# Copies of hash bits and later loads of K, Q and V issued from GpSimd's queue instead of SyncE's

## The chip, the cores and the metric

The kernel runs on one core of a Trainium2 chip. The metric is the device time of one execution in microseconds (us). A core has five engines that work side by side, each through its own list of instructions in order: PE (TensorE, matrix products), DVE (VectorE), ACT (ScalarE), POOL (GpSimd) and SP (SyncE, which here only issues DMA transfers). A DMA is issued by one engine's queue, which first waits for whatever the transfer needs, and is then carried out by 16 DMA engines beside the others. PSUM is the accumulator memory of PE, SBUF the core's main memory.

## The reference

Attention with a mask from hashing, then a two-layer network with an ELU. A score counts only where the six hash bits of the query's and the key's projection agree.

```python
def _attn_ref(q, k, v, proj):          # q, k, v: 4 x 8 x 768 x 64, proj: 64 x 6
    q_bits = (np.einsum('bhsd,dk->bhsk', q, proj) > 0)
    k_bits = (np.einsum('bhsd,dk->bhsk', k, proj) > 0)
    ...
    mask = q_bucket[:, :, :, None] == k_bucket[:, :, None, :]
    scores = scale * np.matmul(q, k.transpose(0, 1, 3, 2))
    scores = np.where(mask, scores, -1000000000.0)
    scores = scores - np.max(scores, axis=-1, keepdims=True)
    attn = np.exp(scores)
    attn = attn / (np.sum(attn, axis=-1, keepdims=True) + 1e-09)
    return np.matmul(attn, v)
...
def _moe_ref(x, w_in, w_out):          # x: 3072 x 512, w_in: 512 x 2048, w_out: 2048 x 512
    h = x @ w_in
    g = np.where(h > 0.0, h, np.exp(np.minimum(h, 0.0)) - 1.0)
    return g @ w_out
```

## The kernel before

**Numbers.** PE multiplies 16-bit floats, so each float32 operand is scaled and split into a high and a low half (`hi`, `lo`), and a product is made of three matmuls or of stacked halves. The weights arrive as 64-bit floats and are decoded in integer steps.

**Units of work.** There are 4 batches of 8 heads. Two heads are a *pair*; a batch is cut into two *chunks* of 3 x 128 query rows, so there are 8 chunks with 4 pairs each, 32 pairs in all. A pair has 6 *slots*, one for each of its two heads and three blocks of 128 queries. The main loop runs over the 192 slots. In each slot PE makes one block of scores (`scores`, L508), DVE takes its maximum on the way out of PSUM (L520, tile `pt`), ACT takes the exponential (L536), ACT and DVE split it into halves (`hl`, L143 and L152), and SP issues a DMA transpose of it into `PT` (L551). Four slots after its last block a pair's product with V runs on PE (`attend`, L559). Beside it runs the network of the chunk before: `h` (L585), its ELU (L596 to L600, tiles `U`), and `o` (L621); at a chunk's end three results are scaled out of PSUM and stored by GpSimd (L635).

**Preparing a pair.** Its Q, and at a batch's first chunk its K too, goes through these steps, each due a set number of slots ahead of the pair's first slot (`PREP`, or `PREP0` for the first four pairs): loads from HBM (`kst` L305, `qst` L344; V is loaded in L391 as `vf`), a sum of squares on ACT that sets the scale (L207), the split (`natk`, `nat1q`, `nat2q`), and DMA transposes on SP into `K1` (L328), `O1` and `O2` (L371, L372). Then `project`: DVE copies the high half of K1 into K2 (L162), PE multiplies by the hash matrix (L286), DVE compares with a threshold (L291, tile `zb`), and the bits are copied by small DMAs of 12 rows x 384 elements into spare rows of K2 (four copies) and O2 (two copies): `bits`, L295. A matmul over these rows then adds the mask to the scores. The traces write K for K1 and K2 and O for O1 and O2.

**What sets the order.** The code emits steps in the order of their due slots. A scheduler at compile time puts them on each engine's list by priority, buffer by buffer and by its own idea of when inputs are there; from slot 30 on PE's list alone is kept as written. Every DMA but the stores and the two loads of the hash matrix stands in SP's list: loads, bits, transposes of K, Q and P, and the weights at the start.

Of the kernel before, what the change touches and what calls it, by code (L numbers as in the profile page):

```python
# [66 lines left out]
def lsh_attention_moe(  # L67
# [10 lines left out]
    nc = tc.nc  # L78
    B, H, S, D = q.shape
    NB = proj.shape[1]  # L80
# [4 lines left out]
    NP = H // 2  # L85
    HALF = S // 2
# [7 lines left out]
    QD = 32  # L94
# [151 lines left out]
    def spare(a, b, dt=F32):  # L246
# [2 lines left out]
        free[0] -= n  # L249
        return Wf[:, free[0] : free[0] + n].bitcast(dt).rearrange("p (a b) -> p a b", b=b)  # L250

    class Stage:


# [21 lines left out]
    def flat(t):  # L276
        return t.rearrange("p a b -> p (a b)")

    def bits(o, ways, w, which):

        t = ps_a.tile([P, 512], F32, tag="av", name="z")[:, :w]
        quads = len(ways[0][1])
        for n, (x, moving) in enumerate(ways):
            for u, mv in enumerate(moving):
                rows = mv.shape[0]
                nc.tensor.matmul(  # L286
                    t[u * QD : (u + 1) * QD], pj["z"][:rows, x, :], mv, start=n == 0, stop=n == len(ways) - 1
                )
        zb = small.tile([P, HALF], F16, tag="zb", name="zb", bufs=2)[:, :w]
        used = slice(0, quads * QD)  # L290
        nc.vector.tensor_scalar(  # L291
            zb[used], t[used], pj["thr"][used, which : which + 1], (MBIT, -MBIT)[which], ALU.is_gt, ALU.mult
        )
        for u in range(quads):
            d = nc.sync.dma_start(o[D : D + 2 * NB, u * w : (u + 1) * w], zb[u * QD : u * QD + 2 * NB])  # L295
        return d

    kexs = {}
# [1 line left out]
    def prep_k(b, ps, sts, sgs):  # L300
        def load():
            with after(0, "first") if b == 0 and "first" in ks[0, 0] else nullcontext():
                for p, st, sg_ in zip(ps, sts, sgs):
                    st["kf"] = stg.tile([P, 2 * NC, D], F32, tag="k", name="kst", bufs=2) if sg_.kf is None else sg_.kf
                    nc.sync.dma_start(  # L305
                        st["kf"].rearrange("p (h c) d -> p h (c d)", h=2),
                        k[b, 2 * p : 2 * p + 2].rearrange("h (p c) d -> p h (c d)", c=NC),
                    )

        def scale():  # L310
            w = len(ps)
            mx = small.tile([P, 2], F32, tag="kx", name="kx")[:, :w]
            for n, (st, sg_) in enumerate(zip(sts, sgs)):
                squares(mx[:, n : n + 1], flat(st["kf"]), sg_.k1)
            yield
            if b not in kexs:
                kexs[b] = small.tile([P, NP], F32, tag="ke", name="ke", bufs=2)
            _, sc = powers(mx, w, 4.0, QK_TOP, "k", squares=True, ex=kexs[b][:, ps[0] : ps[0] + w])
            for n, st in enumerate(sts):
                st["ksc"] = sc[:, n : n + 1]  # L320

        def split(st, sg_):
            s, nat = st["ksc"], sg_.k1
            scaled("n_hi", nat[:, :, :D], st["kf"], s)
            rest("n_lo", nat[:, :, D:], st["kf"], s, nat[:, :, :D])
            st["K1"] = okp.tile([P, 2 * NC, P], F16, tag="K1", name="K1", bufs=NP)
            st["K2"] = okp.tile([P, 2 * NC, P], F16, tag="K2", name="K2", bufs=NP)
            st["first"] = nc.sync.dma_start_transpose(st["K1"], flat(nat))  # L328

        def project(st):  # L330
            k1, k2 = flat(st["K1"]), flat(st["K2"])
            copied("dup", k2[:D], k1[:D])
            quads = [k1[:, u * HALF : (u + 1) * HALF] for u in range(4)]
            st["done"] = bits(k2, ((0, quads), (1, quads)), HALF, 0)

        return load, scale, split, project

    def prep_q(b, c0, nc_, ps, ksts, sts, sgs):
        def load():
            with after(0, "first") if b == 0 and "first" in ks[0, 0] else nullcontext():  # L340
                for p, st, sg_ in zip(ps, sts, sgs):
                    st["qf"] = stg.tile([P, 2 * HC, D], F32, tag="q", name="qst", bufs=2) if sg_.qf is None else sg_.qf
                    st["qf"] = st["qf"][:, : 2 * nc_, :]
                    nc.sync.dma_start(  # L344
                        st["qf"].rearrange("p (h c) d -> p h (c d)", h=2),
                        q[b, 2 * p : 2 * p + 2].rearrange("h (p c) d -> p h (c d)", c=NC)[:, :, c0 * D : (c0 + nc_) * D],
                    )

        def scale():
            w = len(ps)  # L350
            mx = small.tile([P, 2], F32, tag="qx", name="qx")[:, :w]
            for n, (st, sg_) in enumerate(zip(sts, sgs)):
                squares(mx[:, n : n + 1], flat(st["qf"]), sg_.q1[:, : 2 * nc_])
            yield
            ex, sc = powers(mx, w, 4.0, QK_TOP, "q", rows=True, squares=True)
            sg = small.tile([P, 2, 2], F32, tag="sg", name="sg")
            c = D**-0.5 * 2.0 ** (-2 * QK_TOP)
            for x in range(2):
                nc.vector.scalar_tensor_tensor(
                    sg[:, x, :w], ex, c if x == 0 else -c, kexs[b][:, ps[0] : ps[0] + w], ALU.mult, ALU.mult  # L360
                )
            for n, st in enumerate(sts):
                st["qsc"], st["sg"] = sc[:, n : n + 1], sg[:, :, n]

        def split(st, sg_):
            s, nat1, nat2 = st["qsc"], sg_.q1[:, : 2 * nc_, :], sg_.q2[:, : 2 * nc_, :]
            scaled("n_hi", nat1[:, :, :D], st["qf"], s)
            rest("n_lo", nat2[:, :, :D], st["qf"], s, nat1[:, :, :D])
            copied("dup", nat1[:, :, D:], nat1[:, :, :D])
            st["O1"], st["O2"] = o_ring.take(2 * nc_, (b, c0))  # L370
            nc.sync.dma_start_transpose(st["O1"], flat(nat1))  # L371
            nc.sync.dma_start_transpose(st["O2"], flat(nat2))  # L372

        def project(st):
            w = nc_ * P
            o1, o2 = flat(st["O1"]), flat(st["O2"])
            hi, lo = ([x[:, u * w : (u + 1) * w] for u in range(2)] for x in (o1, o2[:D]))
            st["made"] = bits(o2, ((2, hi), (2, lo), (3, lo)), w, 1)

        return load, scale, split, project  # L380


    def prep_v(b):
        st = {"f": [], "v": [None] * NP}

        def load():
            mx = small.tile([P, NP], F32, tag="vx", name="vx")
            for p in range(NP):
                f = vpool.tile([P, 2, NC, D], F32, tag="v", name="vf")
                with tc.issue_after(ks[b, V_AFTER]["done"].ins) if b == 0 else nullcontext():  # L390
                    nc.sync.dma_start(  # L391
                        f.rearrange("p h c d -> p h (c d)"),
                        v[b, 2 * p : 2 * p + 2].rearrange("h (p c) d -> p h (c d)", c=NC),
                    )
                st["f"].append(f)
            st["mx"] = mx
            if b == 0:
                for p in range(NP):
                    sums(p)
# [288 lines left out]
    ks, qs = {}, {}  # L688

    def prep(ns):  # L690

        c = chunks[pairs[ns[0]][0]]
        ps = [pairs[n][1] for n in ns]
        b = c["b"]
        for n in ns:
            qs[n] = {}
        sgs = [stages[n % STAGES] if n < NP else steady for n in ns]
        ksts = [ks.setdefault((b, p), {}) for p in ps]
        parts = [(prep_q(b, c["c0"], c["nc"], ps, ksts, [qs[n] for n in ns], sgs), [qs[n] for n in ns])]
        if c["c0"] == 0:  # L700
            parts.insert(0, (prep_k(b, ps, ksts, sgs), ksts))

        def load():
            for part, _ in parts:
                part[0]()

        made = []

        def sums():
            made.extend(part[1]() for part, _ in parts)  # L710
            for m in made:
                next(m)

        def scale():
            with behind_max():
                for m in made:
                    next(m, None)

        def split(i):
            for part, sts in parts:  # L720
                part[2](sts[i], sgs[i])

        def project(x, i):
            part, sts = parts[x]
            part[3](sts[i])

        return load, sums, scale, split, project, len(parts)
# [7 lines left out]
    for ns in groups:  # L735
        early = ns[0] < NP
        lead = [begin[ns[0]] - x for x in (PREP0 if early else PREP)]
        split_at = []
        for n in ns:
            at = begin[n] - (PREP0 if early else PREP)[2]  # L740

            w = 2 * chunks[pairs[n][0]]["nc"]
# [61 lines left out]
    done = 0  # L804
# [84 lines left out]
    for G in range(starts[-2] + 1):  # L889
        if G == starts[0]:  # L890
            ordered.enter_context(tc.manual_schedule(engines={mybir.EngineType.PE}))
        if G < len(slots):
            n, at = slots[G]
# [61 lines left out]
```

## Time and profile before

| | |
|---|---|
| time, median of 3 runs | 952.47 us (951.82 to 953.67) |
| the profiled execution | 948.24 us, of it the span 946.5 us |
| PE busy, share of the span | 818.4 us, 86% |
| ACT busy | 739.3 us, 78% |
| DVE busy | 704.0 us, 74% |
| POOL busy | 15.7 us, 2% |
| SP's DMA queue, share of 16 engines | 68.9%, 131.25 MB |
| GpSimd's DMA queue | 1.9%, 6.29 MB |

A busy time is the sum of an engine's instructions; waits and the issuing of DMAs are not in it. A row of the timeline reads: start in us from the span's start, duration, engine, line, operation, tile written and tiles read, count; in brackets the idle time before it and what ended it. "SPq" is the queue of SP: its rows are issues, and the time of a row is how long the issue held the queue. A merged row (x2, x4) contains any waits between its members. A row of the waits reads: waiting engine, tile and line, releaser, then total us, times, longest. In a row that gives a line's instructions the three durations are minimum, median and maximum in ns. The first 160 us or so are the head, in which the weights are loaded and decoded and the first chunk's attention runs; then the network of one chunk runs beside the attention of the next, until about 860 us, and the last chunk's network ends the kernel.

### The profile page before, as it was taken

How to read it: one execution, taken by the hardware profiler on the slowest of the kernel's cores; microseconds unless marked ns; L12 is line 12 of the kernel's file. 1: busy time of each engine (PE TensorE's matmuls, PEld its weight loads, DVE VectorE, ACT ScalarE, POOL GpSimd, SP SyncE). 2: the span in 40 equal slices, each digit the busy share in tenths (PEclk: the TensorE clock that was granted, in tenths of full speed). 3: DMA queues.
4: the chain of work that ended last, by engine and by line, in shares of the span. 5: the costliest groups of instructions: out<-in, count | busy, mean ns of one | idle time of the engine just before them, and what ended most of it. 6: DMA issues, size and time to landing. Idle time of an engine off the chain costs nothing.

```text
span 946.5 us, 14531 instructions
## 1 busy us (share of the span) xinstructions
PE 818.4 (86%) x4975; PEld 420.4 (44%) x4975; DVE 704.0 (74%) x1528; ACT 739.3 (78%) x1469; POOL 15.7 (2%) x49
## 2 busy tenths in 40 slices
PE   2536555888999999988998999998999999999996
PEld 0113222444545555444544455544545555555553
DVE  6899899898867877678777687787878687674332
ACT  4677777999879888789779788889888788885442
POOL 1000000000000000000000000000000000000000
PEclk9956666998999999999999999999999999999998
DMA  9999886776887767696886767795777667556000
GB/s 280 280 207 224 226 231 161 136 141 145 153 167 169 153 113 126 132 187 117 163 180 137 139 109 150 148 181 101 144 155 136 118 119 151 102 101 100 34 1 35
DMA packets 404586, 138.47 MB, mean 146 GB/s; under 512 B 380960, under 2 KB 398880, under 8 KB 404512
## 3 DMA queue, kind: packets, MB, share of 16 engines
q1 hardware_dynamic: 402432, 131.25, 68.9%
q0 software_dynamic: 1920, 6.29, 1.9%
q8 instruction: 39, 0.64, 0.3%
q14 instruction: 35, 0.29, 0.1%
q10 hardware_dynamic: 160, 0.00, 0.0%
HBM read 35.65 MB, written 6.29 MB: 44 GB/s over the span
## 4 chain that ended last, share of the span: by engine, by line
issue 50%; DVE 14%; PE 14%; DMA 13%; ACT 6%; SPq 1%; POOL 1%; POOLq 0%; ACTq 0%; DVEq 0%
PE o L621 4%; PE av L559 4%; PE h L585 3%; DVE pt L520 3%; DMA PT<-hl 3%; DVE hl L152 3%; PE s L508 2%; DMA K<-natk 2%; DMA O<-nat1q 2%; ACT pt L536 2%; DMA W<-in_moe_w_in_dram 1%; DMA U<-in_moe_w_out_dram 1%; DVE W L469 1%; POOL out_dram L635 1%; DVE W L479 1%
## 5 line engine op out<-in xcount | busy, mean ns | idle before, releaser
L621 PE MATMUL o<-W,U 128*128 128x512 f16 x1152 | 280.2, 380 | 3.2 <-ACT W L143 3.1
L585 PE MATMUL h<-x,W 128*128 128x384 f16 x1536 | 279.8, 326 | 0.0
L585 PEld LDWEIGHTS <-W 128*128 128x128 f16 x1536 | 147.5, 98 | 111.1 <-issue 9.9
L536 ACT ACTIVATE pt<-pt,nb,sg 128x768 f32<-128x768 f32 x192 | 195.3, 1019 | 1.7
L152 DVE SCALAR_TENSOR_TENSOR hl<-pt,r,hl 128x768 f16<-128x768 f32 x192 | 189.4, 1011 | 7.5 <-ACT hl L143 7.2
L520 DVE TENSOR_SCALAR_CACHE_REDUCE pt<-s 128x768 f32<-128x768 f32 x177 | 168.0, 949 | 22.9 <-PE s L508 21.9
L143 ACT ACTIVATE hl<-pt,r 128x768 f16<-128x768 f32 x192 | 168.7, 927 | 20.2 <-DVE r L546 19.4
L508 PE MATMUL s<-K,O 128*128 128x384 f16 x708 | 153.3, 340 | 32.2 <-DVE pt L520 26.9
L621 PEld LDWEIGHTS <-U 128*128 128x128 f16 x1152 | 111.0, 98 | 122.7 <-issue 8.9
L559 PE MATMUL av<-PT,vhl 128*64 128x384 f16 x1152 | 115.6, 350 | 27.3 <-DMA PT<-hl 20.8
L600 DVE SCALAR_TENSOR_TENSOR U<-U 128x384 f32<-128x384 f32 x128 | 70.9, 554 | 85.8 <-ACT U L599 84.8
L508 PEld LDWEIGHTS <-O 76*128 76x128 f16 (+1 forms) x768 | 74.7, 102 | 134.7 <-issue 51.2
L596 ACT ACTIVATE U<-h,ch 128x384 f32<-128x384 f32 x128 | 72.9, 570 | 63.7 <-PE h L585 63.6
L152 DVE SCALAR_TENSOR_TENSOR U<-U,sgg 128x384 f16<-128x384 f32 x128 | 78.4, 612 | 53.3 <-ACT U L143 53.3
L559 PEld LDWEIGHTS <-vhl 128*64 128x64 f16 x1152 | 72.8, 117 | 81.7 <-ACT hl L143 17.7
L143 ACT ACTIVATE U<-U,sgg 128x384 f16<-128x384 f32 x128 | 77.8, 608 | 20.5 <-DVE U L600 20.4
L599 ACT ACTIVATE U<-h,ch 128x384 f32<-128x384 f32 x128 | 72.9, 570 | 0.0
L472 PE MATMUL acc<-W,ones 128*128 128x512 bf16 x32 | 16.9, 546 | 35.7 <-DVE W L469 35.5
L536 ACT ACTIVATION_READ_ACCUMULATOR pt<-pt,nb,sg 128x1 f32 x192 | 36.4, 190 | 0.0
L533 ACT ACTIVATE nb<-m,sg 128x2 f32<-128x2 f32 x96 | 27.7, 289 | 6.8 <-DVE pt L520 6.4
L291 DVE TENSOR_SCALAR zb<-z,pjt 64x384 f16<-64x384 f32 (+1 forms) x48 | 29.1, 606 | 3.9 <-PE z L286 3.9
L207 ACT ACTIVATE nat1q<-qst 128x384 bf16<-128x384 f32 x30 | 15.5, 516 | 18.1 <-DMA O<-nat1q 16.0
(103 smaller groups left out, 527.2 us busy)
## 6 DMA issues: line engine op xcount, KB each, us to landing
U<-in_moe_w_in_dram SPq DMA_DIRECT2D x12, 512.0 KB
vf<-in_v_dram SPq DMA_DIRECT2D x16, 384.0 KB
U<-in_moe_w_out_dram SPq DMA_DIRECT2D x12, 512.0 KB
out_dram<-W POOLq DMA_DIRECT2D x24, 256.0 KB, 4.0
qst<-in_q_dram SPq DMA_DIRECT2D x30, 192.0 KB
kst<-in_k_dram SPq DMA_DIRECT2D x14, 384.0 KB
PT<-hl SPq DMA_TRANSPOSE x192
W<-in_moe_w_in_dram SPq DMA_DIRECT2D x4, 512.0 KB
```

The lines of the kernel that those rows point to most:

```text
L143: nc.scalar.activation(o, x, AF.Copy, scale=s)
L152: nc.vector.scalar_tensor_tensor(o, x, s, hi, ALU.mult, ALU.subtract)
L291: nc.vector.tensor_scalar(zb[used], t[used], pj["thr"][used, which : which + 1], (MBIT, -MBIT)[which], ALU.is_gt, ALU.mult)
L508: nc.tensor.matmul(s_tile[:, n, :HALF], st[o][:rows, at, :], kst[kk][:rows, j * NC + n * HC : j * NC + (n + 1) * HC, :].rearrange("p a b - ...
L520: top = nc.vector.tensor_scalar(pt.rearrange("p (n e) -> p n e", n=2), s_tile[:, :, :HALF], CLAMP, None, ALU.max, ALU.max, accum_out=duo[0 ...
L536: nc.scalar.activation(pt, pt, AF.Exp, bias=nb[:, n : n + 1], scale=st["sg"][:, 0:1], accum_out=sm[:, n : n + 1])
L559: nc.tensor.matmul(av[j * D : (j + 1) * D], vt[:, j, c, vx, :], PTs[j][:, :, px, c, :], start=n == 0, stop=n == last,)
L585: nc.tensor.matmul(h, WH[:, g * KT + t, wx, fc * P : (fc + 1) * P], c["xs"][t][:, xx, :], start=n == 0, stop=n == 3 * KT - 1,)
L596: nc.scalar.activation(e, h, AF.Exp, scale=c["ch"])
L599: nc.scalar.activation(hp, h, AF.Relu, scale=c["ch"])
L600: nc.vector.scalar_tensor_tensor(e, e, -1.0, hp, ALU.add, ALU.min)
L621: nc.tensor.matmul(o[t][:, :DO], g16[:, gx, t * P : (t + 1) * P], WH[:, NSI + 1 + f, wx, :], start=f == 0 and i == 0, stop=f == NF - 1 and ...
```

## The change

DMAs of three kinds get another issuing queue, GpSimd's in place of SP's: the copies of hash bits, the loads of K and Q, and the loads of V. The first chunk's pairs (n < 4, and K and V of batch 0) keep SP. Nothing is computed differently, and sizes and buffers stay. The new lines make line numbers behind them three higher.

```diff
+    def queue_of(st):
+        return nc.sync if st["early"] else nc.gpsimd
+
...
-    def bits(o, ways, w, which):
+    def bits(o, ways, w, which, queue):
...
-            d = nc.sync.dma_start(o[D : D + 2 * NB, u * w : (u + 1) * w], zb[u * QD : u * QD + 2 * NB])
+            d = queue.dma_start(o[D : D + 2 * NB, u * w : (u + 1) * w], zb[u * QD : u * QD + 2 * NB])
...
-                    nc.sync.dma_start(
+                    queue_of(st).dma_start(
                         st["kf"].rearrange("p (h c) d -> p h (c d)", h=2),
...
-            st["done"] = bits(k2, ((0, quads), (1, quads)), HALF, 0)
+            st["done"] = bits(k2, ((0, quads), (1, quads)), HALF, 0, queue_of(sts[0]))
...
-                    nc.sync.dma_start(
+                    queue_of(st).dma_start(
                         st["qf"].rearrange("p (h c) d -> p h (c d)", h=2),
...
-            st["made"] = bits(o2, ((2, hi), (2, lo), (3, lo)), w, 1)
+            st["made"] = bits(o2, ((2, hi), (2, lo), (3, lo)), w, 1, queue_of(sts[0]))
...
-                    nc.sync.dma_start(
+                    (nc.gpsimd if b else nc.sync).dma_start(
                         f.rearrange("p h c d -> p h (c d)"),
...
-            qs[n] = {}
+            qs[n] = {"early": n < NP}
...
-        ksts = [ks.setdefault((b, p), {}) for p in ps]
+        ksts = [ks.setdefault((b, p), {"early": b == 0}) for p in ps]
```

Since the scheduler orders every engine's list anew, the change moves more than the DMAs. SP's list before, in the second batch, where the third and the fourth of its K tiles are transposed (K_2496 and K_2795 are K1 of its third and fourth pair, K_2176 the K2 of its second; O_ are the Q tiles):

```order
L328 DMA_TRANSPOSE K_2496<-natk 128x12x128
L551 DMA_TRANSPOSE PT<-hl 128x12x128 x2
L295 DMA K_2176<-zb 12x384 x4
L295 DMA O_2182<-zb 12x384 x2
L328 DMA_TRANSPOSE K_2795<-natk 128x12x128
L344 DMA qst<-in_q_dram 128x2x192 x2
L305 DMA kst<-in_k_dram 128x2x384
L551 DMA_TRANSPOSE PT<-hl 128x12x128 x2
L371 DMA_TRANSPOSE O_2801<-nat1q 128x6x128
L372 DMA_TRANSPOSE O_2802<-nat2q 128x6x128
```

The same place of SP's list in the changed kernel:

```order
L331 DMA_TRANSPOSE K_2496<-natk 128x12x128
L554 DMA_TRANSPOSE PT<-hl 128x12x128 x2
L331 DMA_TRANSPOSE K_2795<-natk 128x12x128
L554 DMA_TRANSPOSE PT<-hl 128x12x128 x2
L374 DMA_TRANSPOSE O_2801<-nat1q 128x6x128
```

The six bits copies and the three loads around the transpose of K_2795 are gone from this queue. GpSimd's list held only the 24 stores after its start; in the changed kernel it has at this place:

```order
L298 DMA K_2176<-zb 12x384 x4
L347 DMA qst<-in_q_dram 128x2x192
L298 DMA O_2182<-zb 12x384 x2
L308 DMA kst<-in_k_dram 128x2x384
L394 DMA vf<-in_v_dram 128x2x384
L298 DMA K_2497<-zb 12x384 x4
L638 DMA out_dram<-W 128x512 x2
L298 DMA O_2503<-zb 12x384 x2
L638 DMA out_dram<-W 128x512
```

Copies, loads and stores now stand in one line, and O_2503's copies stand between a chunk's stores. On DVE the same place before, from the split of the fourth pair's K (natk) to the copy into its K2 (K_2796):

```order
L152 SCALAR_TENSOR_TENSOR natk<-kst,ks,natk 128x12x64
L600 SCALAR_TENSOR_TENSOR U<-U 128x384
L546 RECIPROCAL r<-r 128x2
L520 TENSOR_SCALAR pt,m<-s 128x768
L152 SCALAR_TENSOR_TENSOR U<-U,sgg 128x384
L152 SCALAR_TENSOR_TENSOR hl<-pt,r,hl 128x768 x2
L600 SCALAR_TENSOR_TENSOR U<-U 128x384
L642 SCALAR_TENSOR_TENSOR ch<-ve,w0e 128x1
L162 COPY K_2796<-K_2795 64x1536
```

And in the changed kernel:

```order
L152 SCALAR_TENSOR_TENSOR natk<-kst,ks,natk 128x12x64
L549 RECIPROCAL r<-r 128x2
L152 SCALAR_TENSOR_TENSOR U<-U,sgg 128x384
L523 TENSOR_SCALAR pt,m<-s 128x768
L152 SCALAR_TENSOR_TENSOR hl<-pt,r,hl 128x768 x2
L162 COPY K_2796<-K_2795 64x1536
L603 SCALAR_TENSOR_TENSOR U<-U 128x384
L645 SCALAR_TENSOR_TENSOR ch<-ve,w0e 128x1
```

The copy, which needs the transpose of K_2795, has moved ahead of the second U (L600 before, L603 now) and of ch, and the first U has moved ahead of natk.

## The prediction

> **What bounds the kernel now.** I read the page first, for which engine is full in which stretch; then the busy time of each engine in four stretches, which puts a ceiling on any gain; then the waits; then single places in the timeline. The stretches (start and end, then busy us and instructions of each engine, the clock granted to PE, DMA share and GB/s):
>
> ```profile
> 0.00:160.00 160.00, 78.64 (x342) 31.56 (x344) 141.30 (x348) 113.44 (x218) 2.58 (x25) 0.71 0.93 237
> 160.00:240.00 80.00, 68.96 (x409) 35.14 (x406) 69.00 (x148) 71.89 (x146) 0.00 (x0) 0.92 0.69 135
> 240.00:860.00 620.00, 592.32 (x3793) 312.61 (x3791) 467.39 (x991) 518.55 (x1045) 9.88 (x18) 1.00 0.74 140
> ```
>
> In the first 160 us DVE is busy for 141.30: that stretch belongs to DVE, and the change takes no instruction from DVE. From 160 on PE sets the end. It is idle for 80.00 − 68.96 = 11.0 us up to 240 and for 620.00 − 592.32 = 27.7 us up to 860; after 860 nothing that moves is left. So the most that any better feeding of PE can bring is 39 us, and only what a DMA queue causes of it can go. The groups of waits (waiting engine and line, releaser: total us, times, longest) and who issues what:
>
> ```profile
> PE s L508 <- DVE pt L520: 26.9, 28, 3.5
> ...
> PE av L559 <- DMA PT<-hl: 20.8, 11, 6.1
> ...
> DVE K L162 <- DMA K<-natk: 15.5, 10, 3.3
> ...
> L295 SPq DMA_DIRECT2D K<-zb x64: 713/722/1621, 21.3 to 728.6; - x64
> L295 SPq DMA_DIRECT2D O<-zb x64: 714/739/1433, 30.4 to 822.8; - x64
> ...
> L551 SPq DMA_TRANSPOSE PT<-hl x192: 1274/1729/3222, 46.5 to 863.8; - x192
> ```
>
> PE waits mostly for DVE's maximum (L520, which frees the scores' bank) and for transposed P (PT). Both lean on SP's queue, which issues in order: the transposes of P, Q and K, the copies of hash bits and the loads all stand in one line, and one issue holds it for 0.72 to 1.73 us (medians above).
>
> **What goes from SP.** All bits copies but those of the first chunk's pairs: 64 − 16 = 48 into K2 and 64 − 8 = 56 into O2. That is 48 x 0.722 + 56 x 0.739 = 76 us of SP's time. The loads of K, Q and V that go too (12 + 28 + 12) are cheaper to issue. None of this is PE's time; it counts only where a transpose that somebody waits for stands behind it. There are two patterns.
>
> **Pattern 1: K's transpose behind six copies.** The second K of a group, at three of the places where this occurs: the first in full, of the other two the end.
>
> ```profile
> 263.53 3.15 SPq L295 DMA_DIRECT2D K<-zb  x4
> ...
> 263.67 1.00 DVE L152 SCALAR_TENSOR_TENSOR natk<-kst,ks,natk 128x768 f16<-128x768 f32 x1
> ...
> 266.79 1.48 SPq L295 DMA_DIRECT2D O<-zb  x2
> ...
> 268.37 1.30 SPq L328 DMA_TRANSPOSE K<-natk  x1
> ...
> 268.51 0.55 DVE L600 SCALAR_TENSOR_TENSOR U<-U 128x384 f32<-128x384 f32 x1
> ...
> 268.98 0.15 DVE L642 SCALAR_TENSOR_TENSOR ch<-ve,w0e 128x1 f32<-128x1 f32 x1
> ...
> 272.46 0.55 DVE L162 COPY K<-K 64x1536 f16<-64x1536 f16 x1 [3.33 <-DMA K<-natk]
> ...
> 273.94 0.81 PE L508 MATMUL s<-K,O 128*128 128x384 f16 x4 [0.73 <-DVE pt L520]
> ...
> 480.43 0.55 DVE L162 COPY K<-K 64x1536 f16<-64x1536 f16 x1 [2.57 <-DMA K<-natk]
> ...
> 481.91 0.81 PE L508 MATMUL s<-K,O 128*128 128x384 f16 x4 [1.14 <-DVE pt L520]
> ...
> 685.40 0.55 DVE L162 COPY K<-K 64x1536 f16<-64x1536 f16 x1 [2.90 <-DMA K<-natk]
> ...
> 686.88 0.81 PE L508 MATMUL s<-K,O 128*128 128x384 f16 x4 [0.83 <-DVE pt L520]
> ```
>
> The source of the transpose is complete at 263.67 + 1.00 = 264.67, but it is issued at 268.37, behind 3.15 + 1.48 = 4.6 us of copies: 3.7 us late. DVE then stands still for 3.33 us, the maximum behind it comes late, and PE waits 0.73. With the copies gone the transpose goes out up to 3.7 us sooner. The new order takes part of it back: DVE's copy now stands ahead of one U (L600) and one ch, which used to run before it, 0.55 + 0.15 = 0.7 us in all. So 3.33 − 3.7 + 0.7 leaves about 0.3 us of DVE's wait. PE's three waits behind it go: 0.73 + 1.14 + 0.83 = **2.7 us**.
>
> **Pattern 2: P's transpose behind a copy.** Four places where PE waits for PT and a moved copy was issued just ahead of it:
>
> ```profile
> 413.03 0.87 SPq L295 DMA_DIRECT2D O<-zb  x1
> ...
> 419.69 1.62 PE L559 MATMUL av<-PT,vhl 128*64 128x384 f16 x17 [0.70 <-DMA PT<-hl]
> ...
> 438.70 3.06 SPq L295 DMA_DIRECT2D K<-zb  x4
> ...
> 439.64 1.01 DVE L152 SCALAR_TENSOR_TENSOR hl<-pt,r,hl 128x768 f16<-128x768 f32 x1
> ...
> 441.45 1.01 DVE L152 SCALAR_TENSOR_TENSOR hl<-pt,r,hl 128x768 f16<-128x768 f32 x1
> ...
> 441.87 3.35 SPq L551 DMA_TRANSPOSE PT<-hl  x2
> ...
> 448.60 4.79 PE L559 MATMUL av<-PT,vhl 128*64 128x384 f16 x35 [3.14 <-DMA PT<-hl]
> ...
> 620.77 0.90 SPq L295 DMA_DIRECT2D O<-zb  x1
> ...
> 627.70 1.49 PE L559 MATMUL av<-PT,vhl 128*64 128x384 f16 x16 [0.98 <-DMA PT<-hl]
> ...
> 646.71 3.07 SPq L295 DMA_DIRECT2D K<-zb  x4
> ...
> 655.56 1.65 PE L559 MATMUL av<-PT,vhl 128*64 128x384 f16 x18 [2.08 <-DMA PT<-hl]
> ```
>
> At 441.87 the first of two hl was ready at 439.64 + 1.01 = 440.65, so 1.2 us were lost; the second hl was ready at 442.46, and its transpose, with 1.7 us for the one ahead, went out near 443.6: 1.1 us lost, by which 3.14 shrinks. Of the 2.08 I take 0.8, an estimate a little below that 1.1 for the same four copies in front. At the two short ones the copy in front (0.87, 0.90) is as long as the wait (0.70, 0.98), so I take them whole. 0.70 + 1.1 + 0.98 + 0.8 = **3.6 us**. I leave out that the 35 matmuls after the wait at 448.60 took 4.79 us, 137 ns each against 92 where 18 took 1.65: a shorter wait may spare some of that too.
>
> **What comes to GpSimd.** It was empty but for 24 stores. No row shows a 9 KB copy issued there. The nearest are SP's copies (0.72 us to issue) and GpSimd's own 256 KB stores:
>
> ```profile
> L635 POOL DMA_DIRECT2D out_dram<-W x24: 539/542/673, 287.3 to 942.3; - x24
> ...
> DMA to landing us min/median/max: 2.3/4.0/5.3
> ...
> 314.85 0.60 DVE L291 TENSOR_SCALAR zb<-z,pjt 64x384 f16<-64x384 f32 x1
> ...
> 319.10 2.19 SPq L295 DMA_DIRECT2D O<-zb  x2
> ...
> 328.27 0.81 PE L508 MATMUL s<-K,O 128*128 128x384 f16 x4
> ```
>
> I take 0.54 us and 4.0 us, the row of the same queue. The cover is the time from the bits to the first scores that read them: 315.45 to 328.27, or 12.8 us, in one of the tightest pairs. Two copies and a landing need 2 x 0.54 + 4.0 = 5.1 of it, so 7.7 us are spare and the cost on PE is nothing; its upper bound is the slower rival below, its lower bound a further gain, since SP's copy began 3.65 us after the bits were ready. The loads are due 18 slots ahead (PREP). A load that waits for a buffer used to hold the transposes; now it holds copies, with that cover.
>
> DVE's and ACT's order moves in many more rows than the two shown. For waits that this makes I take 1 us back, an estimate: a third of PE's mean wait for L520 (26.9 / 28) at each of three places.
>
> **Sum.** −2.7 − 3.6 + 1.0 = −5.3 us, against the profiled execution's 948.24 (span 946.46 and 1.8 around it): 942.9. That execution lay 4.2 below the median of 952.47, so for a median I carry the difference over: 952.5 − 5.3 = 947.
>
> **Rivals.** *No change.* SP's line is shorter, but what stood behind it waits for something else: P's transposes also wait for a free PT buffer, and the compile-time order calls for DVE's copy sooner, as above. For it speaks that pattern 1's three PE waits are only 2.7 us of 26.9; against it that the transpose gains up to 3.7 us and the order takes back 0.7. It gives −1.9 to +1.9: 950.5 to 954.
>
> *A larger gain.* If PE's waits for PT outside the head go (20.8 − 8.9, the head's part, is 12) and a third of those for L520, the time falls by 12 to 20: 932 to 940. Against it: at most of these places no moved copy stands in front.
>
> ```profile
> PE av L559 <- DMA PT<-hl: 8.9, 3, 6.1
> ...
> PEld L508 <- DMA O<-zb: 16.1, 4, 6.3
> ```
>
> *Slower: GpSimd's line holds the copies past their cover.* At three chunk ends the O copies now stand between out stores, which wait for the chunk's last results. It decides when what stands in front holds GpSimd for more than the 7.7 us, or when one copy takes over (12.8 − 4.0) / 2 = 4.4 us. The price is a wait of PE for O bits, of which the second row (here with SP's copies, in the head) has the longest, 6.3, and a mean of 4. Three places at 4 are 12, at 6.3 they are 19; less the 5.3, that is 7 to 14 slower: 959 to 966. Half of it would be 953. Against it: K's and O's bits come later in DVE's and PE's order than what the loads ahead of them wait for.
>
> The Trainium skill has a rule that speaks for this rival (SBUF — State Buffer, section "SBUF: two separate sides"): GpSimd writes the descriptors of its DMAs itself, and cannot while DVE runs an operation in a two-port mode; it names about 620 ns alone and 3100 ns beside such a copy. Here the 24 stores took 539 to 673 ns beside a DVE that is busy 75% of the time, which does not show it. An estimate from that page's 3.1 us for each of two copies, with the landing above, is 10.2 of the 12.8 us: by the rule alone the sum would stay, and the rival would need a hold of 2.6 us instead of 7.7.
>
> **How the numbers follow.** Forecast (2 to 12 faster) 0.52, no change 0.19, larger gain 0.06, slower rival and other waits of the new order 0.23. The likeliest is 947, with 940 to 950 as its own range. The range runs from 938 (part of the larger gain) to 959 (the near end of the slower one). About 0.2% (1.9 us) is what a measurement of this kernel can tell from no change; by that bound the forecast and the larger gain together are faster (0.58), the second case is the same (0.19), and the last is slower (0.23).
>
> **What would show it.** Right: DVE's wait for K<-natk (15.5) falls under 9; PE's for PT after 240 falls by about 3.6; PE is busy at least 595 of the 620 us from 240 to 860; copies on GpSimd take near 0.54 us. Wrong: PE waits for O<-zb or K<-zb after 200; PE's wait for L520 grows past 27, which would mean that the new order costs more than the shorter line brings; or the head (DVE's 160 us) moves by more than 2 us.

## The result and the profile after

The changed kernel takes 989.36 us (median of 4, 982.36 to 993.57) against 953.07 (median of 4, 951.82 to 955.52) for the kernel before in the same comparison: ratio 1.037, interval 1.0306 to 1.0434. It is 36 us slower. The forecast was 947, with a range of 938 to 959. The profiled execution took 993.57, of it the span 991.8. Of the kernels below, one execution of f1, two of e4 and one of g2 ran in a slower state of the chip: the ratios leave them out, the medians do not, and the traces of e4 and g2 are of such executions.

The busy time by stretch of the changed kernel, in the columns of the prediction's first fence:

```profile
0.00:160.00 160.00, 73.85 (x317) 28.92 (x317) 125.58 (x319) 100.64 (x196) 12.94 (x40) 0.85 0.92 217
160.00:240.00 80.00, 60.12 (x339) 29.95 (x339) 67.48 (x138) 64.62 (x121) 5.95 (x10) 0.82 0.73 145
240.00:860.00 620.00, 573.48 (x3610) 300.00 (x3608) 458.34 (x976) 505.15 (x1020) 84.56 (x148) 0.98 0.74 137
```

The first row is the surprise: in the first 160 us DVE does 125.58 us of work where it did 141.30. The head, which was to stay as it was, has lost 15.7 us. After it PE has lost 592.32 − 573.48 = 18.8 us of the same 620. The groups of waits of the changed kernel (columns as before):

```profile
PE s L511 <- DVE pt L523: 38.5, 27, 6.4
...
DVE K L162 <- DMA K<-natk: 32.2, 11, 5.3
...
ACT natk L207 <- DMA K<-natk: 22.5, 6, 6.3
...
PE av L562 <- DMA PT<-hl: 15.5, 9, 5.6
```

DVE's wait for K's transpose, which was to fall from 15.5 under 9, has doubled. PE's wait for L520 rose from 26.9 to 38.5. Of the waits that the prediction names, only PE's for PT fell (20.8 to 15.5). ACT's wait for K's transpose (its sum of squares writes into the tile that the transpose reads) grew to 22.5; in the kernel before it was

```profile
ACT natk L207 <- DMA K<-natk: 3.0, 3, 1.7
```

The issues themselves (minimum, median, maximum in ns, by line):

```profile
L298 POOL DMA_DIRECT2D O<-zb x56: 497/510/809, 128.8 to 862.7; - x56
L298 POOL DMA_DIRECT2D K<-zb x48: 497/511/540, 250.5 to 765.9; - x48
...
L554 SPq DMA_TRANSPOSE PT<-hl x192: 1274/1705/5018, 53.8 to 906.7; - x192
```

GpSimd issues a copy in 0.51 us, near the 0.54 taken. On SP the median of P's transposes hardly moved (1.73 to 1.71 us), but one of them now holds the queue for 5.0 us (3.2 at most before).

### The profile page after: what moved, and what is told of

Its sections match the earlier page's. It is cut to its first block, busy times and chain, and to the rows that moved or that the text cites. A ratio compares the mean times of both kernels' runs of the same rounds, so it can differ in the third digit from the quotient of the medians.

```text
span 991.8 us, 14622 instructions
## 1 busy us (share of the span) xinstructions
PE 829.1 (84%) x4975; PEld 424.0 (43%) x4975; DVE 707.7 (71%) x1528; ACT 741.2 (75%) x1469; POOL 107.8 (11%) x205
## 4 chain that ended last, share of the span: by engine, by line
PE 29%; DMA 22%; issue 21%; ACT 13%; DVE 13%; SPq 1%; POOL 1%; ACTq 0%; DVEq 0%; POOLq 0%
PE h L588 9%; PE o L624 9%; DMA K<-natk 7%; PE s L511 5%; PE av L562 5%; ACT pt L539 4%; DMA PT<-hl 4%; DMA O<-nat1q 4%; DVE pt L523 3%; DVE hl L152 2%; DMA vf<-in_v_dram 2%; ACT hl L143 2%; DMA W<-in_moe_w_in_dram 1%; ACT W L143 1%; DMA U<-in_moe_w_out_dram 1%
## 5 line engine op out<-in xcount | busy, mean ns | idle before, releaser
L624 PE MATMUL o<-W,U 128*128 128x512 f16 x1152 | 284.4, 383 | 13.3 <-ACT W L143 13.1
L588 PE MATMUL h<-x,W 128*128 128x384 f16 x1536 | 283.4, 329 | 1.5 <-ACT x L571 1.0
L511 PE MATMUL s<-K,O 128*128 128x384 f16 x708 | 155.4, 343 | 42.0 <-DVE pt L523 38.5
L143 ACT ACTIVATE hl<-pt,r 128x768 f16<-128x768 f32 x192 | 168.5, 926 | 15.1 <-DVE r L549 14.3
L562 PE MATMUL av<-PT,vhl 128*64 128x384 f16 x1152 | 115.4, 349 | 27.0 <-DMA PT<-hl 15.5
L603 DVE SCALAR_TENSOR_TENSOR U<-U 128x384 f32<-128x384 f32 x128 | 70.9, 554 | 90.6 <-ACT U L602 89.7
L143 ACT ACTIVATE U<-U,sgg 128x384 f16<-128x384 f32 x128 | 77.7, 607 | 19.2 <-DVE U L603 19.0
L298 POOL DMA_DIRECT2D O<-zb x56 | 28.7, 516 | 257.3 <-DVE zb L294 225.5
L347 POOL DMA_DIRECT2D qst<-in_q_dram x28 | 21.0, 749 | 230.9 <-DVE nat1q L162 111.1
L298 POOL DMA_DIRECT2D K<-zb x48 | 24.3, 514 | 105.7 <-DVE zb L294 105.4
```

What stands on the lines that cost most here:

```text
L143: nc.scalar.activation(o, x, AF.Copy, scale=s)
L298: d = queue.dma_start(o[D : D + 2 * NB, u * w : (u + 1) * w], zb[u * QD : u * QD + 2 * NB])
L511: nc.tensor.matmul(s_tile[:, n, :HALF], st[o][:rows, at, :], kst[kk][:rows, j * NC + n * HC : j * NC + (n + 1) * HC, :].rearrange("p a b - ...
L562: nc.tensor.matmul(av[j * D : (j + 1) * D], vt[:, j, c, vx, :], PTs[j][:, :, px, c, :], start=n == 0, stop=n == last,)
L588: nc.tensor.matmul(h, WH[:, g * KT + t, wx, fc * P : (fc + 1) * P], c["xs"][t][:, xx, :], start=n == 0, stop=n == 3 * KT - 1,)
L603: nc.vector.scalar_tensor_tensor(e, e, -1.0, hp, ALU.add, ALU.min)
```

## The experiments

One view serves most of them: by how much the exponential (ACT L536, one for each of the 192 slots) ends later than in the kernel before, at seven of the 192, one trace of each kernel (in us; the letters stand for the kernels introduced below). Lines are numbered as in the kernel before in all of these, but 8 higher in e4 and g2.

```
no.   before | change  e1    e2  |  f1    f2    f3    f4    g4    h1
  0     41.3 |   7.3   1.2   2.7 |   0.9   3.5   3.7   0.5   1.0   1.1
 24    151.8 |  16.4   1.9  13.9 |   1.0   6.3   4.1   9.8   2.1   1.7
 40    225.1 |  23.4   2.0  21.0 |  -0.1  13.3   9.0  16.9   3.2   0.3
 64    328.8 |  29.5   8.3  21.4 |  -1.3  13.7  13.7  26.9   4.3  -3.0
 96    467.8 |  32.6   8.4  23.2 |  -7.8  12.3  18.9  31.5   3.8  -7.0
136    640.9 |  41.9  14.2  31.0 | -11.6  19.0  25.1  47.3   7.3 -10.0
191    858.8 |  43.1  13.9  34.7 | -10.4  23.2  27.6  49.2   7.1 -10.6
```

### Which DMAs: copies alone, loads alone, late loads, gated loads

The trace of the change suggested one theory: a load on a second queue runs at the same time as the transposes on SP's and delays them. In the head, before and after (timeline: start, duration, and in brackets the wait). The kernel before:

```profile
18.65 0.55 DVE L162 COPY K<-K 64x1536 f16<-64x1536 f16 x1 [0.22 <-DMA K<-natk]
...
38.88 0.47 SPq L305 DMA_DIRECT2D kst<-in_k_dram  x1
```

The changed kernel:

```profile
14.47 2.04 SPq L331 DMA_TRANSPOSE K<-natk  x1
...
14.50 0.84 POOL L308 DMA_DIRECT2D kst<-in_k_dram  x1 [11.01 <-DMA W<-in_k_dram]
...
24.73 0.55 DVE L162 COPY K<-K 64x1536 f16<-64x1536 f16 x1 [5.26 <-DMA K<-natk]
```

The load of the next batch's first K stood at 38.88 in SP's line, behind everything the head needs; on GpSimd it leaves at 14.50, with the first K transpose. The packets on the DMA engines show what then happens. In each us from the start time in the first column, in the changed kernel: packets of the transposes (256 bytes) that start, their mean ns, then GpSimd's load packets of 4608 bytes and their mean ns:

```
16   1040   19     3   279
17    236   29    31   462
18    184   40    17   625
19    244   42    15   694
20     93   36    16  1337
21     30   18    12   616
22     42   18    16   590
```

In the us at 16, with the load hardly under way, 1040 packets of the transposes start; beside the load 30 to 244, and the load's own packets take 279 to 1337 ns, where the shortest of the trace take 175. Counted off in the order of issue, the K transpose puts out its last packet at 22.8, 8.3 us after its issue; the same one in the kernel before, with no load beside it, was issued at 13.95 and took 4.1 us. The Trainium skill (DMA: Bandwidth & Descriptors, section "Queues, rings and completion order") says that each DMA engine takes turns between the queues that have work, one whole packet at a time. This trace agrees in so far as packets of both queues start in every us from 16 to 22; how strictly they take turns it cannot show, since it does not say which DMA engine took a packet. It adds that both sides lose. On the *same* queue this did not happen here: the load of weights that stands behind the K transpose in SP's line, issued at 16.60, has its first packets in the us at 23.

The first four kernels: e1 puts only the copies on GpSimd, e2 only the loads; e3 is the change with the loads of batches 0 and 1 on SP; e4 is the change with a wait ahead of each of GpSimd's loads, a copy of one element of the tile that the last transpose writes (`turned_to`).

```diff
@@ e1 @@
-                    queue_of(st).dma_start(
+                    nc.sync.dma_start(
@@ e2 @@
-            st["done"] = bits(k2, ((0, quads), (1, quads)), HALF, 0, queue_of(sts[0]))
+            st["done"] = bits(k2, ((0, quads), (1, quads)), HALF, 0, nc.sync)
@@ e3 @@
-                    queue_of(st).dma_start(
+                    (nc.gpsimd if b > 1 else nc.sync).dma_start(
...
@@ e4 @@
+        return tc.issue_after(nc.gpsimd.tensor_copy(g, turned_to[0]).ins)
...
+                    with gated(st):
```

> Only the bits copies on GpSimd; all loads of K, Q and V back on SP. Collision theory (the loads on a second queue run between the packets of the transposes and make those land late): the slowdown is gone, and what the prediction counted for the copies stands, 944 to 953 us; DVE's wait for K<-natk under 9 us (before 15.5, after 32.2), the first 100 us as before (DVE busy 84.9 us, after 71.3). Copies theory (copies held in GpSimd's line, or the order that the scheduler makes without them on SP, costs the 36 us): 970 to 990, the head moves little.

> Only the loads of K, Q and V on GpSimd; all bits copies back on SP. Collision theory: as slow as the change or a little slower, 985 to 998 us, the first slot's exponential about 7 us late, DVE's wait for K<-natk above 28 us. Copies theory: 948 to 960.

> As the change, but the loads of K, Q and V of batches 0 and 1 stay on SP, so that GpSimd loads only batches 2 and 3. Collision theory: the loss of the first two batches (after against before: +7 us at slot 0, +23 at slot 40, about +30 at slot 80) goes, that of the later ones (+10 or so) stays, with the gain of the copies at most: 953 to 966 us. Copies theory: 970 to 990. If the loss is in the head alone: 947 to 955.

> As the change, but ahead of each load on GpSimd stands a copy of one element of the tile that the last transpose in program order writes, so that a load starts only when that transpose has landed. Collision theory, with the same buffer release (DVE's split, the last reader of the staging tile) starting both the transpose and the next load: K transposes no longer meet a load, DVE's wait for K<-natk falls from 32.2 to under 20 us, and 15 to 30 us of the 36 come back: 958 to 975. If any other load on a second queue costs the same, since a transpose of P comes every 4 us or so: 978 to 995. Copies theory: no change, 980 to 995.

Measured: e1 964.43 (ratio to before 1.0122, 1.0094 to 1.0149), e2 977.27 (1.0261, 1.0227 to 1.0296), e3 975.38 (1.0243, 1.0209 to 1.0276), e4 1018.73 (1.0596, 1.0525 to 1.0667). Before: 953.03. The two parts add up (11.4 + 24.2 = 35.6 of 36.3), and the loads are the larger. In the head, at no. 24, e2 is 13.9 late and e1 1.9; but each has a list order of its own, and how much of the 13.9 belongs to the loads is settled only with the next kernels. e3 is on time in the head (2.2 late at no. 24, 0.7 at no. 40) and falls behind later (11.7 at no. 96, 24.4 at no. 191): its 975.38 misses the range of the collision theory and lies in that of the copies theory. e1 misses its range too: the copies alone cost 11.4 us, not in the head, and DVE's wait for K<-natk is 16.7, not under 9. e4 did what its gates are for (DVE's wait for K<-natk is 5.5) and is slower than either theory allowed: the gates made loads late (ACT waits 43.6 us for qst and 28.1 for kst), so its time says nothing on the collisions.

e1 shows where its time goes. Around one place, PE's and DVE's timeline (its last row is of another place), then two windows, of which PE's busy time and its clock are to be read:

```profile
289.75 0.51 PE L286 MATMUL z<-K,pjz 128*32 128x384 f16 x8
...
290.32 0.62 DVE L291 TENSOR_SCALAR zb<-z,pjt 128x384 f16<-128x384 f32 x1 [3.57 <-PE z L286]
...
293.10 0.95 DVE L520 TENSOR_SCALAR_CACHE_REDUCE pt<-s 128x768 f32<-128x768 f32 x1
...
294.11 0.82 PE L508 MATMUL s<-K,O 128*128 128x384 f16 x4 [2.44 <-DVE pt L520]
...
400.73 2.44 PE L621 MATMUL o<-W,U 128*128 128x512 f16 x6 [2.26 <-ACT W L143]
```

```profile
292.07:295.48 3.41, 1.37 (x8) 0.84 (x9) 3.41 (x7) 2.75 (x4) 2.34 (x5) 0.96 0.33 114
295.48:298.90 3.42, 3.42 (x15) 1.05 (x13) 2.36 (x6) 3.39 (x9) 0.00 (x0) 0.54 1.03 215
```

No DMA is in this chain. DVE stands 3.57 us at the threshold of K's bits, whose product PE has not yet made, while the maximum that PE needs (L520) waits behind it in DVE's list. In the kernel before, the same two stood the other way round (there the 17th zb of DVE's list follows the 56th maximum, here it precedes it):

```profile
283.86 0.94 DVE L520 TENSOR_SCALAR_CACHE_REDUCE pt<-s 128x768 f32<-128x768 f32 x1
...
286.54 0.61 DVE L291 TENSOR_SCALAR zb<-z,pjt 128x384 f16<-128x384 f32 x1
```

PE then idles 2.44 us, and in the next window its clock is halved (0.54 and not 0.50, since these windows lie 0.3 us beside the clock's own steps). The last row of the timeline is such a place on ACT, where the scaling of a result (L143) came late for its turn. Both are the new *order*, for which the prediction had set 1.0 us.

### The queues in the old order, the order with the old queues

To separate the two, edges hold the lists of PE, DVE and ACT, and of what is left on SP, to the order of the kernel before, instruction by instruction; the DMAs alone change queue (f1: copies, f2: loads, f3: both). f4 is the reverse: the queues of before with the lists of the changed kernel.

```diff
     ordered.close()
...
+    for names in json.loads(zlib.decompress(base64.b85decode(ORDER))):
+        names = [f"I-{n}" for n in names if f"I-{n}" in traced]
+        for x, y in zip(names, names[1:]):
+            tc.add_manual_dep(traced[y], x, edge, reason="order")
```

> Bits copies on GpSimd, loads on SP, and edges that hold the lists of PE, DVE, ACT and what is left on SP to the order of the kernel before. The run with the bits alone was 11.4 us slower than before; its trace shows PE gaps of 1.4 to 2.5 us behind DVE's and ACT's lists, each followed by 3.4 us or more of TensorE at half clock. Order theory (the lists that the compile-time scheduler made, not the copies, cost those 11.4): 944 to 953 us, at most one half-clock stretch between 250 and 860. Copies theory (a copy issued by GpSimd comes later for whoever reads it): 960 to 967.

> Loads of K, Q and V on GpSimd, bits copies on SP, lists of PE, DVE, ACT and the rest of SP in the order of the kernel before. The loads alone were 24.2 us slower. Collision theory (loads on a second queue run between the transposes' packets): 967 to 980, and the head's loss (14 us at slot 32) stays. Order theory: 950 to 960, the head's loss mostly gone.

> The whole change with the lists of PE, DVE, ACT and the rest of SP in the order of the kernel before. Order theory: most of the 36 us gone, 945 to 962. Collision theory: 967 to 982, the head's loss stays. If both hold and add up, it is the run of the loads in the old order less what the copies save.

> The queues of the kernel before, with the lists of PE, DVE, ACT and of the DMAs that stay on SP in the order of the changed kernel. Order theory: a good part of the 36 us is here with no DMA moved, 965 to 985, with half-clock stretches after 250 as in the change. Collision theory: 945 to 960, and no loss in the head.

Measured (before 951.48): f1 947.28 (0.9951, 0.9928 to 0.9973), f2 969.56 (1.0195, 1.015 to 1.024), f3 977.9 (1.0272, 1.0226 to 1.0318), f4 997.02 (1.0478, 1.0435 to 1.052). Both theories hold, each for its part: f1 lies in the range of the order theory, f2 and f3 in that of the collision theory, f4 above both of its ranges. The head's loss did not stay in f2 as expected: at no. 32 e2 is 14.4 late, f2 5.9.

f1: with the order held, the copies win 0.49% or 4.7 us. f1 against e1, which differ in order alone, is 1.7% or 16 us. f1's stretches and waits:

```profile
0.00:160.00 160.00, 79.38 (x338) 31.80 (x340) 140.30 (x346) 112.40 (x216) 5.10 (x29) 0.82 0.95 237
...
240.00:860.00 620.00, 600.68 (x3863) 320.44 (x3863) 473.13 (x998) 523.96 (x1053) 56.26 (x108) 1.00 0.76 142
```

```profile
PE s L508 <- DVE pt L520: 18.3, 21, 4.1
...
DVE K L162 <- DMA K<-natk: 6.3, 6, 2.1
```

The head is back (DVE 140.30), DVE's wait for K is 6.3, PE is busy 600.68 of 620.

f2: no order has changed, and DVE waits longer for K than in any other run but the change itself:

```profile
DVE K L162 <- DMA K<-natk: 30.3, 11, 4.8
PE s L508 <- DVE pt L520: 28.2, 25, 3.5
```

The K transposes after 200 us, from issue to last packet and from first to last packet (mean of 12 in us; the packets are counted off in the order of issue):

```
before 3.43 2.07    f1 3.58 2.28    f2 5.28 3.29    f3 4.87 2.81
g3     3.47 2.12    g4 4.26 2.15    h1 3.47 2.19    change 4.58 2.72
```

f4 shows how much a list costs that was made for other queues: 45.5 us with not one DMA moved. The order is made at compile time from the scheduler's own idea of when each input is there, and there, it seems, ACT's squares stand where GpSimd's early loads would have been in time. One row of its waits (1.1 us in the change):

```profile
ACT natk L207 <- DMA kst<-in_k_dram: 39.3, 7, 12.6
```

The bill of the change, all relative to before: copies −4.7, loads +18.5, both in one GpSimd line 25.9 − (18.5 − 4.7) = +12.1 more, and the new order 36.3 − 25.9 = +10.4. The intervals leave the +12.1 between about 6 and 19 and the +10.4 between about 2 and 18. The last is no constant of the order: it cost 16 us with the copies alone moved (e1 against f1) and 45.5 with nothing moved (f4).

### What of a load does it

Three kernels in the old order. g2 is f2 with a wait ahead of K's loads for the last K transpose, g3 has only V's loads on GpSimd, g4 the loads on ACT's queue.

```diff
@@ g2 @@
+        return tc.issue_after(nc.gpsimd.tensor_copy(g, turned_to[what]).ins)
...
+                    with gated(st["early"], "k"):
@@ g3 @@
-                    queue_of(st).dma_start(
+                    nc.sync.dma_start(
@@ g4 @@
-queue_of = lambda st: nc.sync if st["early"] else nc.gpsimd
+queue_of = lambda st: nc.sync if st["early"] else nc.scalar
...
-                    (nc.gpsimd if b else nc.sync).dma_start(
+                    (nc.scalar if b else nc.sync).dma_start(
```

> As the run of the loads in the old order (969.6 us), but ahead of each K load on GpSimd stands a copy of one element of the K1 tile that the last K transpose in program order writes, so that a K load cannot start before that transpose has landed. Theory of the common release (DVE's split frees the staging tile and starts the transpose, so load and transpose leave together): DVE's wait for K<-natk falls from 30.3 to under 18 us and the time to 953 to 964. If it is any load beside any transpose: 966 to 975, since the loads only move to other transposes.

> Old order, bits on SP; of the loads only the 12 of V on GpSimd, those of K and Q back on SP. Theory of the common release: V's staging tile is not freed by what starts a transpose, so nearly nothing is lost, 949 to 955 us. If every load beside the transposes costs by its bytes (12 x 384 KB of 14.6 MB, about a third of the 18 us): 956 to 961.

> As the run of the loads in the old order, but the loads go through ACT's queue (a hardware queue as SP's, packets of 768 and 1536 bytes) in place of GpSimd's (packets of up to 4608 bytes). If a second queue is enough: K transposes beside a load again take 3 to 4 us from first to last packet (2.0 alone, 3.9 beside GpSimd's loads), and the time is 965 to 985, with 52 x 0.5 = 26 us of issuing on ACT in it. If it is GpSimd's large packets: 2.0 to 2.5 us beside a load, and 950 to 965.

Measured (before 949.77): g2 981.96 (1.0303, 1.0247 to 1.0358), g3 953.03 (1.0037, 1.0016 to 1.0058), g4 956.44 (1.0069, 1.0044 to 1.0094).

g2 is right in the wait and wrong in the time. The waits of g2:

```profile
PE s L516 <- DVE pt L528: 43.1, 30, 9.0
...
ACT natk L207 <- DMA kst<-in_k_dram: 29.7, 8, 6.7
...
DVE K L162 <- DMA K<-natk: 15.2, 10, 3.6
```

DVE's wait for K is halved (30.3 to 15.2): the K loads did leave together with K's transposes, since one split of DVE frees the staging tile and completes the transpose's source. But a load that waits comes late to ACT (29.7; 0.9 in f2), and it meets transposes of P instead, which took 5.7 us from issue to last packet beside a load (15 after 200 us, with 8 or more of its packets), 3.6 without one. SP's line had done both at once: the load right behind the transpose, without a wait. g3 says that V's loads, a third of the bytes, are a fifth of the loss.

g4: through another hardware queue, with packets of 768 and 1536 bytes, the same loads cost 6.6 us and not 18.5, the issuing on ACT included (its row: 12 of the 52):

```profile
L305 ACTq DMA_DIRECT2D kst<-in_k_dram x12: 374/375/397, 19.4 to 632.8; - x12
...
DVE K L162 <- DMA K<-natk: 22.8, 10, 4.8
```

K's packets run 2.15 us, nearly as before (2.07), but start later. So two thirds of the loads' loss go with GpSimd's queue: there the packets run 3.29. Whether that is the packet's size, the moment at which ACT's list issues a load or something else of that queue was not tried.

### The end of the kernel, and both on one line

f1's last exponential is 10.4 us early, but its span only 2.7 us shorter. The rest is in the last instructions: GpSimd ends with a DRAIN, for which all others wait. Its time by number of DMAs that GpSimd had issued:

```
before 24: 3.3    g3 36: 3.8    f2 76: 3.0    f1 128: 11.1    e3 160: 4.0    change 180: 5.5
```

Four kernels, again in the old order: g1 is meant as f1 with the last pair's copies for O2 on SP (126 DMAs), h1 is f1 with the 24 stores on SP, h2 f1 with the last batch's K bits and the last chunk's Q bits on SP, h3 f3 with the loads on ACT's queue.

```diff
@@ g1 @@
-            qs[n] = {"early": n < NP}
+            qs[n] = {"early": n < NP or n == len(pairs) - 1}
@@ h1 @@
-                            nc.gpsimd.dma_start(rows[:, c["c0"] + u, :], ot)
+                            nc.sync.dma_start(rows[:, c["c0"] + u, :], ot)
@@ h2 @@
-            qs[n] = {"early": n < NP}
+            qs[n] = {"early": n < NP or n >= len(pairs) - NP}
...
-        ksts = [ks.setdefault((b, p), {"early": b == 0}) for p in ps]
+        ksts = [ks.setdefault((b, p), {"early": b in (0, B - 1)}) for p in ps]
@@ h3 @@
-                    queue_of(st).dma_start(
+                    (nc.sync if st["early"] else nc.scalar).dma_start(
...
-                    (nc.gpsimd if b else nc.sync).dma_start(
+                    (nc.scalar if b else nc.sync).dma_start(
```

> As the run of the bits copies in the old order, but the last pair's two copies for O2 stay on SP, so that GpSimd issues 126 DMAs in place of 128. In that run the kernel ended with a DRAIN of GpSimd of 11.1 us (3.3 in the kernel before with 24 DMAs, 5.5 in the change with 180). If the drain goes with the number of DMAs as such: no change, 944 to 950 us. If it goes with where the count stops (a full 128): the drain falls to 3 to 6 us and the time to 939 to 944.

> Old order; bits copies on GpSimd as in the run of the bits in the old order (947.3 us), and the 24 stores of the output on SP instead of GpSimd, so that GpSimd issues the 104 copies alone. If the DRAIN of 11.1 us at the end belongs to the small copies: it stays near 11 or is over before the last store lands, since GpSimd is done with its list 100 us earlier; then it is off the path and the time is 937 to 943. If it belongs to the stores behind them: 943 to 950.

> Old order; bits copies on GpSimd except those of the last batch's K and of the last chunk's Q, which stay on SP, so that GpSimd issues 80 copies and 24 stores, and none but stores after about 660 us. If the DRAIN is work left over from the last copies: 3 to 5 us and 939 to 945. If it goes with their number in all or with the ring's state: 8 to 11 us, 945 to 950.

> Old order; bits copies on GpSimd and the loads of K, Q and V on ACT's queue. Bits alone were 0.5% faster, loads on ACT's queue 0.7% slower, loads on GpSimd 2.0% slower, but both on GpSimd 2.7% slower and not 1.5%. If that excess comes of copies and loads standing in one line or ring of GpSimd: the two effects add here, 949 to 956 us. If it comes of having bits and loads beside the transposes at once: 958 to 968.

Measured: g1 946.13 (0.996, 0.9942 to 0.9978; DRAIN 11.1); with before at 952.55, h1 936.96 (0.9841, 0.9814 to 0.9868), h2 945.94 (0.9927, 0.9905 to 0.9949; DRAIN 9.1), h3 956.68 (1.0035, 1.0015 to 1.0055; DRAIN 11.1).

g1 tests nothing: the edit does not reach the copies. Pairs are prepared two at a time and both take the queue of the first (`queue_of(sts[0])`), which is not the last pair. Its trace has GpSimd issue 128 DMAs, 56 copies for O2 among them, as in f1; it is f1 a second time.

h1 is the best version found, 1.6% faster than before. Its DRAIN still takes 9.2 us but begins at 809, when GpSimd's list ends, and lies beside PE's last 120 us. Its stretch and DVE's wait:

```profile
240.00:860.00 620.00, 600.45 (x3868) 319.46 (x3867) 473.23 (x998) 523.89 (x1054) 46.19 (x90) 1.00 0.75 142
```

```profile
DVE K L162 <- DMA K<-natk: 6.7, 7, 2.0
```

h2 speaks against work left over from the last copies: GpSimd's last one went out at 717, 215 us ahead of the DRAIN, which took 9.1 all the same. With 104 DMAs it took 9.1 and 9.2, with 128 (e1, f1, g1, h3) 11.1, but with 76 to 180, loads among them, 3.0 to 5.5. What sets it stays open.

h3 adds up within its interval: −0.5% for the copies and +0.7% for the loads on ACT's queue make +0.2%, measured +0.35%, 0.7 us above the range expected. So the 12.1 us that f3 costs beyond its parts do not come of taking both kinds off SP as such. That they come of copies and loads in one line of GpSimd fits, but loads on GpSimd with copies on a third queue were not run. Not many more transposes of P meet GpSimd's loads in f3 than in f2 (15 and 10), but they take longer, 5.6 us against 4.4 on average; how the line brings that about was not taken apart.

## Why the prediction was wrong, point by point

**The loads, at no cost.** This is the step with the largest miss. The loads that go were costed at nothing, in the head and after it, because SP's issue time was all that was looked at; what the transfer costs the transposes that it now runs beside was left out. Measured, the loads on GpSimd cost 18.5 us (f2), with the copies in the same line 30.6 (f3 less f1). "A load that waits for a buffer used to hold the transposes; now it holds copies" is right about what it holds. But the line of one queue was also a protection: what stood behind a transpose there did not run beside it.

**The head.** "The change takes no instruction from DVE", so the head would stay: wrong, since both the loads and the new order reach it: DVE's 141.30 us of work in the first 160 fall to 134.87 in f2 and to 130.97 in f4. In the old order the loads alone put the slots 6.3 us late by no. 24 and 13.3 by no. 40, the whole change (f3) 4.1 and 9.0. So of the change's 23.4 at no. 40 the other 14.4 came with the new order.

**The new order, +1.0 us.** Mis-sized by ten times: 10.4 us in the change (about 2 to 18), 16 between e1 and f1. The estimate took mean waits of PE for L520 at three places. It missed that DVE's and ACT's lists were made against other arrival times, so that any instruction, here L291 and the scaling of results (L143), may come to stand in front of the one that PE needs; and that an idle stretch has a second price, the clock (below). The prediction's own sign for this case came true: PE's wait for L520 grew past 27, to 38.5.

**Pattern 1, −2.7 us.** The mechanism was right, and too small: in f1 DVE's wait for K<-natk fell from 15.5 to 6.3, below the predicted 9, and between 240 and 860 PE's wait for L520 from 16.6 to 7.5. That is 9.1 us where three waits of 2.7 in all were counted.

**Pattern 2, −3.6 us.** Right at its four places, and undone at four others. PE's waits of 0.70, 3.14, 0.98 and 2.08 are 0.44, 0.91, 0.48 and 0.88 in f1: 4.2 us less. But PE's wait for PT between 240 and 860 is 8.9 in all (7.5 before), since 6.2 of it stand at four other places, of 2.45, 1.08, 1.17 and 1.45 (before 0.6 there together). At each of these the transpose of P ran beside stores and copies of GpSimd and took 6.9 to 7.6 us from issue to last packet; before, beside stores alone, the same four took 5.2 to 5.8, and in h1, beside copies alone, 4.0 to 4.4. In h1 the four waits are gone and the total is 3.8. The prediction's slower rival had chunk ends in view, but for a late copy and not for a slow transpose.

**GpSimd's copies at no cost.** Right for whoever reads them: 0.52 us to issue, a median of 3.4 to landing in f1 (0.54 and 4.0 taken), and no wait of PE for bits after 200 in f1, h1 or the change. Nor was GpSimd's issuing held up in the change, beside a DVE that is busy 71% of the span: 0.81 us at most for a copy. Not thought of: the stores' transfers just named, and the DRAIN, which takes 7.8 of f1's gain back.

**The rivals.** Slower was given 0.23, by copies held past their cover, which did not happen, or by other waits of the new order, which did; its price was 7 to 14 us. No rival had a load beside a transpose.

**The sum.** −5.3 us is near what the copies alone bring in the old order (f1, −4.7), and that is luck: pattern 1 brought more than was counted, pattern 2 was undone, the order was held, and the DRAIN took 7.8 back. The loads, 52 of the 156 DMAs that move and nearly all of their bytes, are not in the sum at all.

## What to carry to other kernels

A queue that issues in order also keeps its transfers apart: before a load is taken off it, ask which transfers it will now run beside, above all when one event releases both. Where a compile-time scheduler orders the engines, measure a moved DMA once with the old order held; here the copies brought 4.7 us in the old order, and the order made for them cost 16. The end of the kernel belongs to the sum: an engine that is given DMAs may need its own time to finish.

## What the runs showed of the hardware

**A PE wait of 2 us costs more than 2 us.** The granted clock changes in steps of 3.41 us. In the 17 traces, between 200 and 860 us, each full-clock window with under 1.42 us of PE work was followed by one or more at half clock, and none with over 1.61. The kernel before had 13.7 us at half clock between 200 and 880, the change 27.3, e1 34.1, f1 and h1 6.8. Since half the clock is lost in it, e1's extra 27.3 against f1 are up to 13.7 of the 16 us. The Trainium skill (TensorE: Matmul & The Clock Gate, section "What's actually happening") has the window of 3413 ns and the halved clock after an idle window; the traces agree on both, but a window 38% busy already counts as idle here (1.30 us in e1's window above, by the clock's own steps; 1.37 in the row). So PE waits of 2 us or so within one window reach that edge: between 240 and 860 the longest for L520 was 1.8 before and 3.1 in the change, the mean 0.8 and 1.3.

**A transpose and a load on two queues hold each other up.** The K transpose issued at 14.47 in the changed kernel needed 8.3 us to its last packet (4.1 before), and the load issued at 14.50 landed at 23.2, after 8.7 us (the quickest of the 12 took 3.9, the median 5.7). Whether one after the other would have been quicker is not shown: with 3.4 us for a K transpose, the mean before, that makes 7.3 to 9.1.
